# Attention and two matrix chains on one core: W13 built by two blocks of rows at a time, with w_out's last blocks beside it

## Chip, core and metric

The kernel runs on one core of a Trainium2 chip. The metric is the time of one execution in device microseconds (us). TensorE does the matrix products into PSUM, VectorE and ScalarE work on SBUF and PSUM, GpSimd on SBUF, and SyncE's queue (SP) starts most transfers.

## What is computed

Eight batches of 576 tokens with eight heads of 64 go through a two-step attention over 32 packed queries, then through two matrix chains in float32. The part that matters here is the first chain, whose `w3` and `w_out` are multiplied first (W13 = w3 @ w_out), since nothing stands between them:

```python
def sm_attn(qq, kk, vv): ...          # softmax(scale * qq @ kk.T) @ vv
p_packed = sm_attn(p, k, v)
out = sm_attn(q, p_packed, p_packed)
x = out as [4608, 512]
a = x @ w1                            # [4608, 1024]
b = x @ w2
h = a * b @ w3                        # w3 [1024, 1024]
x = h @ w_out                         # w_out [1024, 512]
h = x @ w_in                          # w_in [512, 2048]
g = np.maximum(0.01 * h, h)
return g @ w_out2
```

The weights arrive as 64-bit words and are turned into float32 on the chip.

## The kernel before

TensorE multiplies rounded float32 operands, so each operand is kept as a high and a low part: ScalarE copies the value into the rounded type (high), another engine subtracts (low), and each product takes three passes, high by high, high by low, low by high (`three`, L102). The subtract is one call, `sub` (L107), on the engine that it is given.

The start of the run, some 182 us, is written out by hand in `SCRIPT` (L11), a list of steps. A step is a letter and its indices, looked up in the table at L738. The steps:

- `k q v p` load attention inputs, `s e n t y` are the first attention step, `S E N` the second, `X`/`x` split its result into the tile AT (L258), `X` with the subtract on VectorE and `x` on GpSimd.
- `l`, `c`, `d` bring in a block of weights by the key `w` (w1, w2), `o` (w_out) or `3` (w3): `l` loads 64-bit words into one of three c64 tiles on SP's queue (L292), `c` begins the conversion, one operation on ScalarE (L276) and two on VectorE (L278, L282), and `d` ends it with an addition on GpSimd (L285). The words then lie in one of six c32 tiles until they are split.
- `o`/`O` split a block of w_out into two tiles of 256 columns (`split_wo1`, L508), `H`/`h` a block of w3 into one wsp tile of 512 columns, of which there are four (`split_half`, L386); the capital O and the small h are on GpSimd, the others on VectorE.
- `M` and `a` make M, w1 and w2 folded with the packed attention (L423, L437); `A` followed by the indices fc, batch and half multiplies M with AT into two PSUM tiles, which ScalarE (L473) and VectorE (L475) take out and multiply. The batch 0 and batch 1 results go to memory.
- `W` followed by fc and h is `w13_half` (L519): 24 matmuls over four of w_out's eight blocks, jc 0 to 3 for h = 0 and 4 to 7 for h = 1, into two of the four PSUM tiles named mm. After h = 1 both are copied and split into W13. Block i of w3 is number 2 fc + h, so W10 needs the split H2, and W01 needs H1 and w_out's blocks 4 to 7.

Before, W13 goes from W00 to W01, W10, W20, W30, W21, W11 and so on; all of w_out is split ahead of W00. The kernel is built with `schedule_with_timeline_sim=True` (L1049): the order of instructions on each engine is fixed when the kernel is built, by a planner with modelled times. The script gives the priority; an engine with nothing else to do takes a later step, so the order on an engine can run ahead of the script.

After the script come alternating stages for four pairs of batches (`x2_stage`, `ab_stage`, L767 to L773) and the second chain (L983 on). These are not touched.

Of the kernel before, what the change touches and what calls it, by code (L numbers as in the profile page):

```python
# [7 lines left out]

SCRIPT = """k0 p0 k1 lw0 v0 s0 v1 cw0 e0 q0 n0 s1 q1 t0 e1 lw1 n1 y0 t1 p1 k2 dw0 S0 y1 cw1 k3 v2 E0 S1 s2 v3 dw1 lw2 N0 E1 e2 q2 X0 N1 n2 s3 t2 q3 X1 e3 cw2 lw3 n3 y2 t3 dw2 M00 S2 lw4 a00 y3 cw3 lw5 S3 dw3 Z M01 a01 A000 E2 cw4 lw6 A001 dw4 cw5 E3 dw5 M02 a02 A100 N2 lw7 A101 cw6 x2 M10 a10 A200 N3 dw6 cw7 A201 x3 lw8 dw7 M03 a03 A010 cw8 lw9 A011 dw8 lo0 M11 a11 A300 cw9 lw10 A301 dw9 co0 M04 a04 A110 cw10 lw11 A111 dw10 do0 M12 a12 A400 cw11 lw12 A401 dw11 lo1 O0 M05 a05 A210 cw12 lw13 A211 dw12 co1 M13 a13 A500 cw13 lw14 A501 dw13 lo2 do1 M06 a06 A310 cw14 lw15 A311 dw14 O1 co2 M14 a14 A600 cw15 lo3 A601 dw15 do2 co3 M07 a07 A410 O2 lo4 do3 A411 co4 lo5 M15 a15 A700 O3 l30 do4 A701 co5 lo6 c30 M16 a16 A510 o4 l31 do5 d30 A511 co6 c31 o5 M17 a17 A610 p2 lo7 do6 d31 A611 o6 l33 co7 l35 A710 H0 h1 do7 c33 p3 A711 o7 k4 d33 c35 l32 H3 d35 l37 c32 H5 d32 l34 c37 H2 k5 d37 c34 l38 k6 l315 d34 H4 h7 s4 c38 d38 W00 l36 c36 l39 l310 d36 h6 c39 l311 H8 e4 l312 W01 t4 W10 W20 s5 c311 v4 k7 d39 l313 d311 c310 c312 e5 c313 d310 h9 W30 v5 d312 H11 W21 h10 s6 l314 W11 n4 c314 d313 d314 q4 v7 W31 y4 t5 W40 s7 H12 q5 W41 h13 W50 n5 e6 v6 c315 d315 n6 H14 t6 W51 y5 e7 H15 y6 W60 n7 W61 W70 W71"""  # L11
KQ = {"k": 1}
F32 = mybir.dt.float32
F32R = mybir.dt.float32r
# [18 lines left out]
def tile_kernel(ctx, tc, qT, kT, vL, pT, w12, w3b, wo1, win, wo2, out):  # L33
# [718 lines left out]
    }  # L752
    for x in SCRIPT.split():
        if x[0] in "lcd":
# [298 lines left out]
```

## Time and profile before

| | |
|---|---|
| median of 3 runs | 1363.2 us (1353.9 to 1364.24) |
| profiled execution | 1353.83 us |
| its span, first to last instruction | 1351.5 us |
| TensorE busy | 1314.0 us, 97% |
| VectorE busy | 934.9 us, 69% |
| ScalarE busy | 690.7 us, 51% |
| GpSimd busy | 183.6 us, 14% |
| mean granted TensorE clock | 0.994 |

The profile is of one execution. The page gives busy times of the whole span; the same by stretches of time shows where an engine is full or idle. PE is TensorE's matmul, PEld its weight load, DVE VectorE, ACT ScalarE, POOL GpSimd, SP SyncE. A granted clock of 1.00 is 2.4 GHz, 0.50 is 1.2 GHz. An instruction that waits for a port inside its run shows as a longer instruction, not as idle time.

### The profile page before, as it was taken

To read this page: it belongs to the slowest core of one execution; us is meant where nothing else is said; L and a number is where in the kernel's file an instruction comes from. 1 tells how busy PE (TensorE), PEld (TensorE's weight loads), DVE (VectorE), ACT (ScalarE), POOL (GpSimd) and SP (SyncE) were. 2 spreads that over 40 slices of the span, in tenths; PEclk is the share of its full clock that TensorE was granted. 3 is DMA by queue.
4 is the path that set the end of the run, shared out by engine and by line. 5 is a ranking of instruction groups with operands and counts; after the bars stand their busy time and mean duration, and the time that the engine had idled before them with its cause. 6 is when DMAs were issued, how large, how long until landed. Compare 5 with 4: busy or idle time off the path is not lost. (4 is left out here: it accounts for less than half of the span.)

```text
span 1351.5 us, 23575 instructions
## 1 busy us (share of the span) xinstructions
PE 1314.0 (97%) x8576; PEld 1248.6 (92%) x8576; DVE 934.9 (69%) x1574; ACT 690.7 (51%) x1345; POOL 183.6 (14%) x146
## 2 busy tenths in 40 slices
PE   6998999999999999999999999999999999999998
PEld 3777999999999999999999999999999999999998
DVE  5988558675977587762977665846665468586667
ACT  4554464665476556644665555545334334344432
POOL 1554422332033212100000000000000000000000
PEclk9998999999999999999999999999999999999999
DMA  9788677668976774387878877467545754778884
GB/s 322 266 280 275 210 228 248 222 213 240 311 246 203 255 245 149 111 304 249 296 273 289 305 264 248 160 213 247 186 146 204 242 192 158 268 264 309 285 295 152
DMA packets 174836, 323.48 MB, mean 239 GB/s; under 512 B 22657, under 2 KB 93313, under 8 KB 174721
## 3 DMA queue, kind: packets, MB, share of 16 engines
q1 hardware_dynamic: 153984, 300.74, 66.4%
q10 hardware_dynamic: 20736, 21.24, 4.6%
q8 instruction: 67, 1.10, 0.3%
q14 instruction: 49, 0.39, 0.1%
HBM read 226.75 MB, written 95.16 MB: 238 GB/s over the span
## 5 line engine op out<-in xcount | busy, mean ns | idle before, releaser
L105 PE MATMUL mm<-AT,M 128*128 128x288 f32 x1536 | 230.5, 302 | 9.2 <-DVE ab L475 5.5
L105 PEld LDWEIGHTS mm<-AT,M 128*128 128x128 f32 x1536 | 210.1, 190 | 27.8 <-DVE ab L475 8.1
L908 PE MATMUL b<-xh,wi 128*128 128x384 f32 x768 | 219.2, 338 | 6.3 <-DMA xh<-xfd 3.8
L908 PE MATMUL b<-gh,wo 128*128 128x384 f32 x768 | 213.9, 336 | 1.4 <-DVE o L871 1.4
L105 PEld LDWEIGHTS mm<-ab,W 128*128 128x128 f32 x1536 | 204.3, 188 | 6.7 <-issue 5.2
L105 PE MATMUL mm<-ab,W 128*128 128x288 f32 x1536 | 210.0, 297 | 0.4 <-DVE ab L475 0.4
L908 PEld LDWEIGHTS b<-xh,wi 128*128 128x128 f32 x768 | 141.6, 189 | 8.6 <-DMA xh<-xfd 3.3
L908 PEld LDWEIGHTS b<-gh,wo 128*128 128x128 f32 x768 | 140.3, 188 | 2.1 <-issue 1.0
L908 PE MATMUL b<-xl,wi 128*128 128x384 f32 x384 | 129.3, 337 | 0.0
L908 PE MATMUL b<-gl,wo 128*128 128x384 f32 x384 | 128.6, 335 | 0.0
L680 ACT CAST gh<-gr 128x1152 fp32r<-128x1152 f32 (+1 forms) x72 | 75.6, 1052 | 67.4 <-PE b L908 32.2
L908 PE MATMUL c<-gh,wo 128*128 128x384 f32 x384 | 107.3, 336 | 0.6 <-DVE o L866 0.5
L908 PE MATMUL c<-xh,wi 128*128 128x384 f32 x384 | 106.4, 336 | 1.4 <-DMA xh<-xfd 1.4
L108 DVE TENSOR_TENSOR gl<-gr,gh 128x1152 fp32r<-128x1152 f32 (+1 forms) x72 | 87.4, 1219 | 22.5 <-ACT gh L680 22.5
L285 POOL TENSOR_TENSOR c<-cT,c 128x512 int32<-128x512 int32 x56 | 76.6, 1369 | 158.4 <-DVE cT L282 75.7
L108 DVE TENSOR_TENSOR M<-m,M 64x512 fp32r<-64x512 f32 (+1 forms) x111 | 75.1, 684 | 23.3 <-ACT M L415 19.4
L680 ACT CAST gh<-gs 128x1152 fp32r<-128x1152 f32 (+1 forms) x54 | 56.9, 1055 | 62.7 <-PE b L908 33.5
L108 POOL TENSOR_TENSOR wsp<-wsp 128x512 fp32r<-128x512 f32 x48 | 64.3, 1347 | 160.1 <-ACT wsp L383 138.2
L108 DVE TENSOR_TENSOR ab<-ab,ab 128x288 fp32r<-128x288 f32 x128 | 65.3, 535 | 29.1 <-ACT ab L454 28.6
L856 ACT ACTIVATE gr<-gr 128x1152 f32<-128x1152 f32 (+1 forms) x54 | 57.3, 1062 | 45.8 <-DVE gr L871 45.5
L868 ACT COPY gr<-b 128x384 f32<-128x384 f32 x96 | 45.8, 478 | 60.0 <-PE b L908 58.4
L475 DVE TENSOR_TENSOR ab<-mm,a 128x288 f32<-128x288 f32 x128 | 57.1, 450 | 24.1 <-ACT a L473 12.7
(144 smaller groups left out, 2385.2 us busy)
## 6 DMA issues: line engine op xcount, KB each, us to landing
xh<-xfd SPq DMA_DIRECT2D x126, 384.0 KB, 5.5
xl<-xfd SPq DMA_DIRECT2D x126, 384.0 KB, 5.2
part<-o SPq DMA_DIRECT2D x48, 384.0 KB, 2.8
o<-part SPq DMA_DIRECT2D x48, 384.0 KB, 4.0
c<-wo SPq DMA_DIRECT2D x24, 512.0 KB, 4.6
wsp<-w12d SPq DMA_DIRECT2D x48, 256.0 KB, 3.0
abd<-ab ACTq DMA_DIRECT2D x80, 144.0 KB, 3.0
ab<-abd SPq DMA_DIRECT2D x80, 144.0 KB, 3.9
```

The costliest lines, as they stand in the source:

```text
L105: nc.tensor.matmul(dst, lhs(i), rhs(j), start=first and n == 0, stop=last and n == 2)
L108: engine.tensor_tensor(out=out, in0=x, in1=rd(hi), op=ALU.subtract)
L285: return lambda: nc.gpsimd.tensor_tensor(out=q, in0=t.bitcast(I32), in1=q, op=ALU.add)
L475: nc.vector.tensor_tensor(out=t, in0=pb[:, :TH], in1=a, op=ALU.mult)
L680: nc.scalar.copy(hi[step], x[step])
L856: nc.scalar.activation(out=out, in_=x, func=AF.Prelu, alpha=0.01)
L868: nc.scalar.copy(out, ps)
L908: nc.tensor.matmul(dst, lhs(l), rhs(r), start=first and n == 0, stop=last and n == total - 1, skip_group_check=True)
```

## The change

Only `SCRIPT` differs. Both scripts have 305 steps with the same loads, conversions, products and splits.

- X2 and X3 in place of x2 and x3, o0 to o3 in place of O0 to O3: these subtracts go from GpSimd to VectorE. H1 in place of h1, and ahead of A711 besides H0 now H2 and H1. Of the sixteen w3 splits three are on GpSimd (h5, h10, h11), before six (h1, h6, h7, h9, h10, h13).
- W13's order is W00 W10 W01 W11, W20 W30 W21 W31, W40 W50 W41 W51, W60 W70 W61 W71. The w3 blocks are loaded, converted and split in this order.
- The loads, conversions and splits of w_out's blocks 4 to 7 (lo4, co4, do4, o4 and on) stand between those of the first four w3 blocks; co7, do7 and o7 come behind W00.
- The steps of the next batches' attention (k4, s4, e4 and on) stand at other places among the W steps.

```diff
 ... dw5 M02 a02 A100 N2 lw7 A101 cw6
-x2 M10 a10 A200 N3 dw6 cw7 A201 x3 lw8 dw7 M03
+X2 M10 a10 A200 N3 dw6 cw7 A201 X3 lw8 dw7 M03
...
-O0 M05 a05 A210 cw12 lw13 A211 dw12 co1 M13 a13 A500 cw13 lw14 A501 dw13 lo2 do1 M06 a06 A310 cw14 lw15 A311 dw14 O1 co2 M14
+o0 M05 a05 A210 cw12 lw13 A211 dw12 co1 M13 a13 A500 cw13 lw14 A501 dw13 lo2 do1 M06 a06 A310 cw14 lw15 A311 dw14 o1 co2 M14
...
-A410 O2 lo4 do3 A411 co4 lo5 M15 a15 A700 O3 l30 do4 A701 co5 lo6 c30
-M16 a16 A510 o4 l31 do5 d30 A511 co6 c31 o5 M17 a17 A610 p2 lo7 do6 d31 A611 o6 l33 co7 l35
-A710 H0 h1 do7 c33 p3 A711 o7 k4 d33 c35 l32 H3 d35 l37 c32 H5 d32 l34 c37 H2 k5 d37 c34
-l38 k6 l315 d34 H4 h7 s4 c38 d38 W00 l36 c36 l39 l310 d36 h6 c39 l311 H8 e4 l312 W01 t4 W10 W20
-...
-s7 H12 q5 W41 h13 W50 n5 e6 v6 c315 d315 n6 H14 t6 W51 y5 e7 H15 y6 W60 n7 W61 W70 W71
+A410 o2 l30 do3 A411 c30 l32 M15 a15 A700 o3 d30 c32 A701 lo4 H0 l31
+M16 a16 A510 d32 co4 lo5 A511 do4 H2 c31 M17 a17 A610 o4 p2 co5 d31 l33 A611 do5 lo6 c33
+A710 o5 H1 co6 d33 p3 A711 W00 do6 lo7 o6 H3 k4 l34 co7 W10 do7 l36 c34 o7 k5 d34 W01
+H4 c36 l35 s4 d36 W11 H6 e4 k6 c35 l37 d35 W20 h5 t4 c37 l38 s5 v4 d37 W30 H7 e5 c38 l310 k7 d38 W21
+...
+H14 y5 e7 v7 c313 l315 d313 W60 H13 y6 c315 n7 d315 W70 H15 W61 W71
```

## Rows read from the trace of the kernel before

**Rows 1.** The page's first part: busy us, share of the span, instructions of each engine.

```profile
PE 1314.0 (97%) x8576; PEld 1248.6 (92%) x8576; DVE 934.9 (69%) x1574; ACT 690.7 (51%) x1345; POOL 183.6 (14%) x146
```

**Rows 2.** Busy time by stretches: start:end, length, each engine's busy us, PEclk, DMA share, GB/s.

```profile
40.00:64.00 24.00, 23.01 (x163) 19.02 (x162) 23.80 (x45) 12.70 (x28) 12.93 (x10) 0.98 0.75 260
64.00:93.00 29.00, 26.75 (x187) 21.43 (x186) 21.07 (x33) 15.11 (x36) 18.14 (x16) 1.00 0.83 271
93.00:112.00 19.00, 17.14 (x117) 13.22 (x115) 19.00 (x31) 12.19 (x28) 11.15 (x9) 1.00 0.80 258
112.00:117.00 5.00, 2.33 (x15) 1.84 (x14) 5.00 (x8) 1.07 (x3) 2.13 (x2) 0.92 0.97 313
117.00:123.00 6.00, 6.00 (x22) 4.59 (x24) 5.97 (x10) 2.99 (x6) 2.62 (x2) 0.50 0.97 349
126.50:182.00 55.50, 55.50 (x476) 51.58 (x475) 28.54 (x57) 27.25 (x67) 20.42 (x15) 1.00 0.64 207
```

**Rows 3.** Groups of instructions, 38 to 126.5 us: busy us, mean ns, idle before.

```profile
L105 PE MATMUL mm<-AT,M 128*128 128x288 f32 x384 | 61.6, 312 | 7.8 <-DVE ab L475 4.1 <-DVE M L108 2.5 <-POOL AT L108 1.0
L282 DVE SCALAR_TENSOR_TENSOR cT<-c,cT 128x512 uint32<-128x512 uint32 x27 | 24.7, 913 | 0.2
L285 POOL TENSOR_TENSOR c<-cT,c 128x512 int32<-128x512 int32 x16 | 21.6, 1352 | 21.5 <-DVE cT L282 15.4 <-ACT a L473 4.3 <-ACT M L440 1.8
L278 DVE TENSOR_SCALAR cT<-c 128x512 uint32<-128x512 uint32 x26 | 19.2, 740 | 4.7 <-DMA c<-wo 3.7 <-DMA c<-w 1.0
L285 POOL TENSOR_TENSOR w<-cT,w 128x512 int32<-128x512 int32 x11 | 15.9, 1463 | 13.1 <-ACT w L276 6.9 <-DMA w12d<-w 2.7 <-DVE cT L282 1.8
L108 POOL TENSOR_TENSOR ab<-c,ab 128x256 fp32r<-128x256 f32 x8 | 7.0, 894 | 3.1 <-ACT ab L513 3.1
L108 DVE TENSOR_TENSOR ab<-c,ab 128x256 fp32r<-128x256 f32 x8 | 5.8, 748 | 0.0
L108 POOL TENSOR_TENSOR AT<-a,AT 128x576 fp32r<-128x576 f32 x2 | 3.0, 1511 | 0.5 <-ACT AT L261 0.5
L108 POOL TENSOR_TENSOR wsp<-c,wsp 128x512 fp32r<-128x512 f32 x1 | 1.8, 1752 | 0.0
```

**Rows 4.** Timeline where TensorE waits: start us, us, engine, line, operation, idle before.

```profile
55.77 0.68 ACT L261 CAST AT<-a 128x576 fp32r<-128x576 f32 x1
56.43 1.30 DVE L278 TENSOR_SCALAR cT<-c 128x512 uint32<-128x512 uint32 x1
57.40 1.60 POOL L108 TENSOR_TENSOR AT<-a,AT 128x576 fp32r<-128x576 f32 x1
59.05 1.31 PE L105 MATMUL mm<-AT,M 128*128 128x288 f32 x8 [0.99 <-POOL AT L108]
...
93.02 0.60 DVE L108 TENSOR_TENSOR ab<-c,ab 128x256 fp32r<-128x256 f32 x1
...
111.00 1.83 DVE L108 TENSOR_TENSOR ab<-c,ab 128x256 fp32r<-128x256 f32 x2
113.83 1.58 PE L105 MATMUL mm<-AT,M 128*128 128x288 f32 x10 [1.13 <-DVE M L108]
114.52 1.59 POOL L285 TENSOR_TENSOR c<-cT,c 128x512 int32<-128x512 int32 x1 [1.97 <-DVE cT L282]
114.90 1.49 DVE L278 TENSOR_SCALAR cT<-c 128x512 uint32<-128x512 uint32 x1
116.81 3.25 PE L105 MATMUL mm<-AT,M 128*128 128x288 f32 x12 [1.40 <-DVE ab L475]
```

**Rows 5.** Timeline of VectorE at 104 us, with no GpSimd instruction beside these.

```profile
104.19 0.41 DVE L278 TENSOR_SCALAR cT<-c 128x512 uint32<-128x512 uint32 x1
104.52 0.41 DVE L108 TENSOR_TENSOR ab<-c,ab 128x256 fp32r<-128x256 f32 x1
105.22 0.68 DVE L282 SCALAR_TENSOR_TENSOR cT<-c,cT 128x512 uint32<-128x512 uint32 x1
```

**Rows 6.** Timeline of TensorE inside the W13 stage.

```profile
134.22 8.29 PE L105 MATMUL mm<-ab,wsp 128*128 128x256 f32 x68
```

More of the change, by code (lines that the diff above doesn't have):

```diff
@@ L7 @@
 from concourse.masks import make_identity
-SCRIPT = """k0 p0 k1 lw0 v0 s0 v1 cw0 e0 q0 n0 s1 q1 t0 e1 lw1 n1 y0 t1 p1 k2 dw0 S0 y1 cw1 k3 v2 E0 S1 s2 v3 dw1 lw2 N0 E1 e2 q2 X0 N1 n2 s3 t2 q3 X1 e3 cw2 lw3 n3 y2 t3 dw2 M00 S2 lw4 a00 y3 cw3 lw5 S3 dw3 Z M01 a01 A000 E2 cw4 lw6 A001 dw4 cw5 E3 dw5 M02 a02 A100 N2 lw7 A101 cw6 x2 M10 a10 A200 N3 dw6 cw7 A201 x3 lw8 dw7 M03 a03 A010 cw8 lw9 A011 dw8 lo0 M11 a11 A300 cw9 lw10 A301 dw9 co0 M04 a04 A110 cw10 lw11 A111 dw10 do0 M12 a12 A400 cw11 lw12 A401 dw11 lo1 O0 M05 a05 A210 cw12 lw13 A211 dw12 co1 M13 a13 A500 cw13 lw14 A501 dw13 lo2 do1 M06 a06 A310 cw14 lw15 A311 dw14 O1 co2 M14 a14 A600 cw15 lo3 A601 dw15 do2 co3 M07 a07 A410 O2 lo4 do3 A411 co4 lo5 M15 a15 A700 O3 l30 do4 A701 co5 lo6 c30 M16 a16 A510 o4 l31 do5 d30 A511 co6 c31 o5 M17 a17 A610 p2 lo7 do6 d31 A611 o6 l33 co7 l35 A710 H0 h1 do7 c33 p3 A711 o7 k4 d33 c35 l32 H3 d35 l37 c32 H5 d32 l34 c37 H2 k5 d37 c34 l38 k6 l315 d34 H4 h7 s4 c38 d38 W00 l36 c36 l39 l310 d36 h6 c39 l311 H8 e4 l312 W01 t4 W10 W20 s5 c311 v4 k7 d39 l313 d311 c310 c312 e5 c313 d310 h9 W30 v5 d312 H11 W21 h10 s6 l314 W11 n4 c314 d313 d314 q4 v7 W31 y4 t5 W40 s7 H12 q5 W41 h13 W50 n5 e6 v6 c315 d315 n6 H14 t6 W51 y5 e7 H15 y6 W60 n7 W61 W70 W71"""
@@ new lines @@
+SCRIPT = """k0 p0 k1 lw0 v0 s0 v1 cw0 e0 q0 n0 s1 q1 t0 e1 lw1 n1 y0 t1 p1 k2 dw0 S0 y1 cw1 k3 v2 E0 S1 s2 v3 dw1 lw2 N0 E1 e2 q2 X0 N1 n2 s3 t2 q3 X1 e3 cw2 lw3 n3 y2 t3 dw2 M00 S2 lw4 a00 y3 cw3 lw5 S3 dw3 Z M01 a01 A000 E2 cw4 lw6 A001 dw4 cw5 E3 dw5 M02 a02 A100 N2 lw7 A101 cw6 X2 M10 a10 A200 N3 dw6 cw7 A201 X3 lw8 dw7 M03 a03 A010 cw8 lw9 A011 dw8 lo0 M11 a11 A300 cw9 lw10 A301 dw9 co0 M04 a04 A110 cw10 lw11 A111 dw10 do0 M12 a12 A400 cw11 lw12 A401 dw11 lo1 o0 M05 a05 A210 cw12 lw13 A211 dw12 co1 M13 a13 A500 cw13 lw14 A501 dw13 lo2 do1 M06 a06 A310 cw14 lw15 A311 dw14 o1 co2 M14 a14 A600 cw15 lo3 A601 dw15 do2 co3 M07 a07 A410 o2 l30 do3 A411 c30 l32 M15 a15 A700 o3 d30 c32 A701 lo4 H0 l31 M16 a16 A510 d32 co4 lo5 A511 do4 H2 c31 M17 a17 A610 o4 p2 co5 d31 l33 A611 do5 lo6 c33 A710 o5 H1 co6 d33 p3 A711 W00 do6 lo7 o6 H3 k4 l34 co7 W10 do7 l36 c34 o7 k5 d34 W01 H4 c36 l35 s4 d36 W11 H6 e4 k6 c35 l37 d35 W20 h5 t4 c37 l38 s5 v4 d37 W30 H7 e5 c38 l310 k7 d38 W21 H8 n4 c310 l39 s6 v5 d310 W31 h10 y4 q4 t5 c39 l311 d39 W40 H9 s7 v6 c311 l312 q5 d311 W50 h11 n5 e6 c312 l314 d312 W41 H12 t6 c314 l313 n6 d314 W51 H14 y5 e7 v7 c313 l315 d313 W60 H13 y6 c315 n7 d315 W70 H15 W61 W71"""
```

## The prediction

> **What bounds the kernel now.** I read the page's first part, then busy time by stretches, then one table of instruction groups for the script's part of the run, and last the timelines of the places where TensorE waits. The page shows TensorE busy 97% of the span, so no other engine can be the bound over the whole [rows 1]. By stretches the loss is found in one place: ahead of 117 us TensorE is idle in every stretch read, most from 93 on, while in the W13 stage, 126.5 to 182, it is busy 55.50 of 55.50 [rows 2]. The reader should see two things in that table. First, the stage that the change reorders most (W13) has no idle TensorE time to give back. Second, ahead of it VectorE is full: 23.80 of 24 us, later 19.00 of 19, 5.00 of 5, 5.97 of 6; only from 64 to 93 has it 7.9 us free.
>
> The table of groups names who TensorE waits for between 38 and 126.5: 7.8 us in all, 4.1 for L475 (the product that empties a's and b's PSUM tiles), 2.5 for the subtract that makes M's low part, both on VectorE, and 1.0 for a subtract on GpSimd [rows 3]. So VectorE, not TensorE, sets the pace there. And VectorE is stretched by GpSimd: L282 takes 0.913 us in the mean and 0.68 alone, L278 0.740 and 0.41 alone [rows 3, 5]. The worst place is 112 to 117, where TensorE is busy 2.33 of 5 us; right behind it, 117 to 123, the granted clock is 0.50, that is 1.2 instead of 2.4 GHz, though TensorE is busy all of it [rows 2]. The idle time (2.67 us) and half of the slow stretch (3.0 us) make 5.7 us lost at one spot. Of the rest of the idle time, 0.99 us is the wait for GpSimd's X3 [rows 4]. The idle time before 40 us stays out: the two scripts are the same up to cw6.
>
> **The splits that move to VectorE.** X2 and X3 are one subtract of 128x576 each, o0 to o3 two of 128x256 each, H1 one of 128x512. Alone, VectorE takes 0.41 us for 256 columns and 0.68 for 512 [rows 5]; 576 columns by the same slope are an estimated 0.75 (the 512 columns are L282's, which also reads two operands from SBUF). The sum added ahead of W00: 2 x 0.75 + 8 x 0.41 + 0.68 = 5.5 us. The ScalarE copies that come before each subtract stay where they are. GpSimd loses 3.0 + 7.0 + 1.8 = 11.8 us of the same work [rows 3].
>
> What does VectorE get back? Its L278, L282 and o-splits are stretched by 26 x 0.33 + 27 x 0.233 + 8 x 0.338 = 17.6 us, over GpSimd's 21.6 + 15.9 + 7.0 + 3.0 + 1.8 = 49.3 us of work, or 0.36 us for each us of GpSimd [rows 3, 5]. 11.8 us less gives back 4.2 us. Net, VectorE gets 1.3 us more, at bounds of 5.5 more (nothing comes back, since the 27 additions of L285 stay and may do the blocking instead) and 6.3 less (each us of GpSimd blocks one). I take 1.3, from the mean over 49 us. By place: X2, X3 and o0 fall into the full stretch up to 64 and there add 2.3 us against some 5 us of GpSimd taken away (1.8 back); o1 to o3 add 2.5 us where 7.9 us are free; H1's 0.68 stands against 1.8 us of GpSimd (0.6 back). So I count the net at nothing in TensorE's time. The cover is the free time from 64 to 93; without it the 1.3 us would be paid one to one.
>
> One row bears on how the blocking works: L278 at 114.90 takes 1.49 us instead of 0.41 while GpSimd adds from 114.52 to 116.11 [rows 4, 5]. The Trainium skill, "SBUF — State Buffer", section "Who interferes with whom", says that VectorE and GpSimd share a port pair that one of them holds for a whole instruction, while the other is blocked. The row agrees; by the rule alone VectorE could win back up to 11.8 - 5.5 = 6.3 us, by the mean it loses 1.3.
>
> **X3's own wait.** A010 and A011 want the AT tile's low part at 58.06 (59.05 less the 0.99 of idle time) and get it at 59.05, since GpSimd begins X3 only at 57.40, though its copy is done at 56.45 [rows 4]. On VectorE X3 would be ready at 56.45 too; VectorE is then inside a stretched L278 until 57.7, so X3 would end about 58.4. TensorE then waits 0.4 instead of 1.0: 0.6 us gained, bounds 0 and 1.0.
>
> **w_out's last four.** co4 to co7 and o4 to o7 go from ahead of the w3 blocks to among them, co7 and o7 to between W10 and W01. Work per block is the same, loads and SP issues too: 12 loads of 512 KB stand ahead of k4's in either script, so SP's queue reaches the second half's k, v, q loads no later. What matters is what VectorE does at 109 to 117. There it runs o7's two subtracts, 1.83 us, right ahead of the M split for which A610 waits 1.13 us, then a stretched L278 ahead of the two L475 for which A611 waits 1.40 us [rows 4]. With o7 gone from this spot, M's split could start up to 1.8 us earlier; that would take A610's wait away and perhaps the slow clock, up to 5.7 us. Against it: the planner lets VectorE run ahead of the script, as o4's first subtract shows, at 93.02, though the script has it behind M16 and A510, while A610's matmuls run at 113.83 [rows 4, 5]. So the next conversion or H split would fill the gap, with its own GpSimd addition behind it. Bounds 0 and 5.7; I take 2, nearer the low end because of that row.
>
> **W13's new order.** W00 W10 W01 W11 needs H0, H2, then o4 to o7 with H1, H3. Each W is 24 matmuls of 8.29 us / 68 = 0.122, so 2.9 us; the stage's 384 run without idle time today [rows 2, 6]. Two blocks hold all four "mm" tiles, so W10 waits for A711's last L475, hidden by W00, and W20 waits for fc 0's two copies and two subtracts, the subtracts 0.41 us each [rows 5], hidden by W11's 2.9 us. Without that cover two subtracts a pair would show, 0.8 us, 3.3 in all four pairs. Four wsp tiles hold H0, H2, H1 and H3 and come free one W at a time, as they do today. Cost: 0, no gain either.
>
> **Sum.** 0 - 0.6 - 2.0 + 0 = -2.6 us. The profiled execution's own time is 1353.8 (span 1351.5), so 1351.2 for it. The median of the runs shown, 1363.2, lies 9.4 us above the profiled one, inside their spread (1353.9 to 1364.2); for the median I say 1360.6.
>
> **The rivals.**
> - The stall clears. Without o7 and with fewer GpSimd instructions, 112 to 123 runs at full clock: -0.6 - 5.7 = -6.3, with all waits of the stretch gone at most -7.8 - 3.0 = -10.8. For it: the 1.83 us stand right before the first wait. Against: VectorE stays full. 1357 (1352 at the least).
> - Slower: VectorE is the bound ahead of W13 and the 5.5 us are paid. It decides when less than 5.5 / 11.8 = 0.47 us comes back for each us taken off GpSimd and no free time lies beside it; the trace has 0.36, so net it goes that way by 1.3 us, and only the free time from 64 to 93 hides it. If nothing comes back: +5.5, and with the slow clock as long again +3.0: +8.5, 1371.7. The Trainium skill, "Perfetto Trace Analysis", section "Identifying the Most-Contended Engine", has the busiest engine relieved first; by this VectorE, full in four stretches, is the wrong engine to load. The rows agree on which engine is full.
> - W01 starves: o7's chain (load, conversion, addition, two subtracts) is last in line and W01 stands still until it ends. Two W ahead of it instead of one give 5.9 us of cover rather than 2.9; o7's subtracts end at 112.8 today [rows 4], so it would have to come 19 us later to cost anything (126.5 + 5.9 - 112.8 = 19.6); at 30 us later 10.4 us are lost, with a slow-clock stretch of 3: 1377.
> - The change does little: the planner runs ahead of the script in both, and the same GpSimd additions fall on the same VectorE work: 1363.
>
> **How the numbers follow.** Small gain 0.45, stall clears 0.17, no difference 0.13, VectorE pays 0.18, W01 starves 0.07. The likeliest gives 1360.6, by itself 1357 to 1363. The range takes in the stall clearing with runs at the low end of their spread (1353.9 - 5 = 1349) and VectorE paying nearly in full (1370); the rest is left out. A change of under 1% (13.6 us) is about what a measurement of this kernel can't tell from none. No case but W01 starving passes that by itself; all idle time and slow clock together are 10.8 us. Faster by over 1% needs the clearing case and low runs: 0.07. Slower by over 1%: W01, or VectorE paying with a longer slow stretch: 0.07. Within: 0.86.
>
> **What would show it.** X3: no GpSimd AT subtract, and A010's wait under 0.5 us. Splits: GpSimd near 37 us instead of 49 between 38 and W00, L278 and L282 closer to 0.41 and 0.68. w_out: o7 behind W00's start, and the clock of the stretch ahead of W00 at 1.00 (gain) or 0.50 again (none). W13: TensorE busy throughout. I am wrong if TensorE idles inside W13, if the wait sum ahead of W00 goes over 10 us, or if something moves behind 182 us, which I left as it is.

## The result

The changed kernel takes 1371.3 us in the median of 13 runs (1364.5 to 1376.4) beside 1361.9 us of the kernel before in 13 runs (1353.9 to 1367.1). The ratio is 1.007, with a 95% interval of 1.0052 to 1.0087: about 9.4 us slower. The prediction said 1360.6 us and a range of 1349 to 1370, so the direction was wrong and the time lies above the range, though it is still within 1%. The interval also shows that this measurement can tell 0.7% from nothing, which the prediction doubted.

The profiled execution of the kernel before was among its fastest, that of the changed kernel a middling one (span 1368.9 us). The two profiles therefore lie 17.4 us apart, more than the kernels do. 4.6 us of this lie ahead of A000, which starts at 40.2 us before and at 44.8 us after. The kernels below that have unit 4 (explained further down) at the front, before among them, start A000 anywhere from 40.2 to 45.0 us, so this part doesn't go with it. Another 6.1 us lie behind the second pair's M, where no step was moved; that stretch takes 1114 to 1126 us in the sixteen profiles, with no clear tie to the order.

The first part of the page, and busy time by stretches (columns as in [rows 2]; the last two rows are the W13 stage and the first x2 stage):

```profile
PE 1316.3 (96%) x8576; PEld 1248.4 (91%) x8576; DVE 949.4 (69%) x1587; ACT 690.3 (50%) x1345; POOL 167.1 (12%) x133
```

```profile
60.00:64.00 4.00, 1.15 (x10) 0.45 (x6) 4.00 (x3) 1.49 (x5) 3.46 (x3) 1.00 0.99 275
64.00:67.00 3.00, 1.59 (x10) 1.36 (x10) 3.00 (x9) 0.74 (x2) 0.00 (x0) 0.85 0.99 381
67.00:73.00 6.00, 5.00 (x20) 3.69 (x20) 4.22 (x9) 0.93 (x3) 0.00 (x0) 0.50 0.13 42
...
112.00:117.00 5.00, 4.21 (x29) 3.36 (x30) 4.97 (x8) 3.06 (x7) 2.57 (x2) 1.00 0.69 216
117.00:123.00 6.00, 5.11 (x31) 3.30 (x28) 5.94 (x11) 2.21 (x7) 2.55 (x2) 1.00 0.88 282
132.70:187.92 55.22, 54.66 (x467) 51.19 (x465) 37.19 (x67) 28.09 (x65) 20.58 (x15) 1.00 0.69 222
187.92:248.37 60.45, 57.74 (x443) 52.85 (x442) 45.32 (x81) 28.73 (x73) 12.79 (x9) 1.00 0.73 234
```

The first x2 stage before, in the same view:

```profile
181.83:237.13 55.30, 55.30 (x421) 51.62 (x420) 45.01 (x82) 27.88 (x67) 15.65 (x10) 1.00 0.84 259
```

The stall of 112 to 123 us is gone: TensorE is busy 4.21 of 5 and 5.11 of 6 us at full clock, where before it had 2.33 us and then 6 us at 0.50 [rows 2]. But a new stall of the same kind stands at 60 to 73 us. TensorE is busy 2.74 of 7 us, and behind that the granted clock is 0.50 (1.2 GHz) for 6 us. And the first x2 stage, which was full, is now 5.2 us longer and has 2.7 us of idle time. The W13 stage is as long as it was.

The places where TensorE waits in the changed kernel (start us, us, engine, line, operation, idle before):

```profile
50.53 3.44 PE L105 MATMUL mm<-AT,M 128*128 128x288 f32 x22 [0.77 <-DVE M L108]
64.13 1.59 PE L105 MATMUL mm<-AT,M 128*128 128x288 f32 x10 [2.98 <-DVE AT L108]
67.18 1.33 PE L105 MATMUL mm<-AT,M 128*128 128x288 f32 x4 [1.46 <-ACT AT L261]
69.33 2.29 PE L105 MATMUL mm<-AT,M 128*128 128x288 f32 x8 [0.82 <-DVE AT L108]
...
146.15 1.68 PE L105 MATMUL mm<-ab,wsp 128*128 128x256 f32 x12 [0.56 <-DVE W L108]
200.39 0.33 PE L219 MATMUL at<-ident,pp 128*128 128x128 f32 x1 [1.48 <-ACT pp L218]
```

A010 and A011 now wait 5.26 us in three pieces for batch 1's AT (L261 copies it, L108 makes the low part), where before one wait of 0.99 us stood [rows 4]. In the same stretch of the kernel before, there is something else on TensorE and on SP's queue, which the prediction's rows don't show:

```profile
34.02 0.33 SPq L129 DMA_DIRECT2D raw<-kT  x1
...
45.46 1.19 PE L167 MATMUL at<-raw,ppad 128*64 128x288 f32 x8
55.09 0.75 PE L198 MATMUL at<-ident,P 128*128 128x128 f32 x4
55.68 0.27 PE L199 MATMUL at<-ident,P 128*64 128x128 f32 x1
```

These are k4, s4 and t4: the loads, scores and transpositions of attention unit 4, the first of the second pair of batches. In the script before, k4 and s4 stand ahead of W00 and t4 behind it, but the planner ran them some 70 to 90 us ahead of W00's start, among the first A steps. In the changed kernel the loads come at 112.87 us and the scores at 119.47 us. The script of the change puts k4 to t4 up to three W later, and the planner no longer takes them to the front.

### The profile page after: what moved, and what is told of

Its sections match the earlier page's. It is cut to its first block, busy times and chain, and to the rows that moved or that the text cites. A ratio compares the mean times of both kernels' runs of the same rounds, so it can differ in the third digit from the quotient of the medians.

```text
span 1368.9 us, 23566 instructions
## 1 busy us (share of the span) xinstructions
PE 1316.3 (96%) x8576; PEld 1248.4 (91%) x8576; DVE 949.4 (69%) x1587; ACT 690.3 (50%) x1345; POOL 167.1 (12%) x133
## 4 chain that ended last, share of the span: by engine, by line
PE 75%; DMA 12%; DVE 9%; ACT 2%; issue 2%; SPq 1%; POOL 0%; ACTq 0%; DVEq 0%; POOLq 0%
PE mm L105 25%; PE b L908 24%; PE c L908 12%; PE a L908 6%; DMA xh<-xfd 3%; PE m L105 2%; PE at L167 2%; DMA part<-o 2%; DMA wsp<-w12d 2%; DVE cT L278 1%; PE at L216 1%; DMA wi<-wid 1%; DMA c<-w 1%; DMA xfd<-PT 1%; DVE cT L282 1%
## 5 line engine op out<-in xcount | busy, mean ns | idle before, releaser
L105 PE MATMUL mm<-AT,M 128*128 128x288 f32 x1536 | 230.9, 301 | 17.3 <-DVE ab L475 4.4
L105 PEld LDWEIGHTS mm<-AT,M 128*128 128x128 f32 x1536 | 209.0, 189 | 37.7 <-issue 8.1
L105 PE MATMUL mm<-ab,W 128*128 128x288 f32 x1536 | 211.1, 296 | 1.2 <-DVE ab L108 0.9
L105 PEld LDWEIGHTS mm<-ab,W 128*128 128x128 f32 x1536 | 204.6, 188 | 8.0 <-issue 6.3
L108 DVE TENSOR_TENSOR gl<-gr,gh 128x1152 fp32r<-128x1152 f32 (+1 forms) x72 | 87.4, 1218 | 22.1 <-ACT gh L680 22.0
L108 DVE TENSOR_TENSOR ab<-ab,ab 128x288 fp32r<-128x288 f32 x128 | 66.9, 549 | 45.1 <-ACT ab L454 44.5
L108 DVE TENSOR_TENSOR M<-m,M 64x512 fp32r<-64x512 f32 (+1 forms) x111 | 75.3, 686 | 20.8 <-ACT M L415 16.4
L108 POOL TENSOR_TENSOR wsp<-wsp 128x512 fp32r<-128x512 f32 x48 | 62.2, 1303 | 172.7 <-ACT wsp L383 142.8
L908 PEld LDWEIGHTS c<-xh,wi 128*128 128x128 f32 x384 | 69.9, 188 | 5.0 <-DMA xh<-xfd 4.3
```

Source lines behind the costliest of these rows:

```text
L105: nc.tensor.matmul(dst, lhs(i), rhs(j), start=first and n == 0, stop=last and n == 2)
L108: engine.tensor_tensor(out=out, in0=x, in1=rd(hi), op=ALU.subtract)
L908: nc.tensor.matmul(dst, lhs(l), rhs(r), start=first and n == 0, stop=last and n == total - 1, skip_group_check=True)
```

## The experiments

All differ from one of the two kernels in the order of `SCRIPT` or the engine of a few splits only; the work is the same. Each time is the median of 6 to 13 runs, the ratio is to the kernel before on the same chip, with its 95% interval. "Unit 4" is the start of its scores, and "A to M" the time from A000's first product to the second pair's M, both from one profiled execution.

| kernel | us | ratio | unit 4, us | A to M, us |
|---|---|---|---|---|
| before, beside after | 1361.9 | 1 | 45.5 | 196.9 |
| after | 1371.3 | 1.0070 (1.0052 to 1.0087) | 119.5 | 203.5 |
| x_only | 1360.4 | 1.0004 (0.9990 to 1.0019) | 47.3 | 195.7 |
| o_only | 1358.2 | 0.9975 (0.9958 to 0.9992) | 48.5 | 193.6 |
| order_only | 1369.2 | 1.0060 (1.0036 to 1.0083) | 116.0 | 202.2 |
| after_x | 1367.5 | 1.0057 (1.0037 to 1.0076) | 116.4 | 206.3 |
| w_order | 1361.9 | 1.0021 (1.0002 to 1.0039) | 49.7 | 200.7 |
| wout_early | 1369.0 | 1.0081 (1.0057 to 1.0106) | 142.5 | 202.1 |
| att_old | 1356.0 | 0.9977 (0.9961 to 0.9993) | 47.2 | 191.6 |
| att_new | 1366.2 | 1.0053 (1.0035 to 1.0070) | 139.7 | 202.3 |
| grp_early | 1354.6 | 0.9962 (0.9944 to 0.9980) | 49.9 | 190.8 |
| rest_early | 1366.2 | 1.0042 (1.0023 to 1.0061) | 117.9 | 199.1 |
| unit4_early | 1356.9 | 0.9978 (0.9962 to 0.9995) | 47.3 | 191.4 |
| grp_late | 1371.4 | 1.0082 (1.0062 to 1.0101) | 137.6 | 203.0 |
| k4_ahead_lo7 | 1356.4 | 0.9979 (0.9958 to 1.0001) | 45.7 | 194.7 |
| k4_behind_l32 | 1362.7 | 1.0022 (1.0007 to 1.0036) | 119.3 | 199.1 |

**First: are the splits to blame?** x_only and o_only make one part of the change alone, on the kernel before.

```diff
 x_only, on before
-x2 ... x3
+X2 ... X3
 o_only, on before
-O0 ... O1 ... O2 ... O3
+o0 ... o1 ... o2 ... o3
```

> The kernel before with X2 and X3 on VectorE and nothing else changed. Theory A (the AT chain comes late: with X2 and X3 on VectorE, the changed kernel's TensorE waits 2.98 + 1.46 + 0.82 us for AT ahead of A010 and A011): 4 to 7 us slower than before, with AT waits of 3 us or more. Theory B (VectorE pays for the subtracts that it takes over, each microsecond one to one): 1.5 us slower. Theory C (the loss comes from the order of the W13 steps and of what stands beside them): no difference, within 1 us.

> The kernel before with o0 to o3 on VectorE and nothing else changed. Theory A: no difference, within 1 us. Theory B: 3.3 us slower, and VectorE full for longer ahead of W00. Theory C: no difference.

X2 and X3 on VectorE change nothing that can be measured. The wait for X3, though, grew: x_only has 1.81 us where before it was 0.99 us [rows 4], so the 0.6 us of the prediction aren't there either. ScalarE's copy is done at 60.85 us, but VectorE comes to the subtract only at 62.20, behind two L278, and it takes 1.27 us beside a GpSimd split:

```profile
60.17 0.68 ACT L261 CAST AT<-a 128x576 fp32r<-128x576 f32 x1 [2.50 <-DVE a L255]
61.22 1.63 POOL L108 TENSOR_TENSOR ab<-c,ab 128x256 fp32r<-128x256 f32 x2 [0.85 <-ACT ab L513]
62.20 1.27 DVE L108 TENSOR_TENSOR AT<-a,AT 128x576 fp32r<-128x576 f32 x1
63.52 1.31 PE L105 MATMUL mm<-AT,M 128*128 128x288 f32 x8 [1.81 <-DVE AT L108]
```

o0 to o3 on VectorE gain 3.4 us (0.25%, 1 to 6 by the interval), and in o_only's profile the clock stays at 1.00 from 112 to 128 us. order_only and after_x take the splits back out of the changed kernel:

```diff
 order_only, on after          after_x, on after
-X2 X3 o0 o1 o2 o3            -X2 X3
+x2 x3 O0 O1 O2 O3            +x2 x3
```

> The changed kernel with x2, x3 and O0 to O3 back on GpSimd: the new order of W13, of w_out's last four blocks and of the attention steps, with H1 on VectorE, remains. Theory A: as the kernel before within 2 us. Theory B: 0.7 us slower than before (H1). Theory C: 5 to 9 us slower than before, with TensorE waiting in the first 20 us behind W13 (1.48 us for pp, 0.93 and 0.29 for ab in the changed kernel).

> The changed kernel with x2 and x3 back on GpSimd and nothing else undone. Theory A: 4 to 7 us faster than the changed kernel, so 2 to 5 us slower than before. Theory B: 1.5 us faster than the changed kernel, so 8 slower than before. Theory C: as the changed kernel, 9 us slower than before.

Both stay at 1.006, so neither theory about VectorE holds: the loss is in the order. The AT waits shrink (in after_x from 5.26 to 0.80 us in all), yet the time hardly moves: after_x idles 5.40 us in the first x2 stage, where the changed kernel idles 2.71.

**Then: which part of the order?** Three things were reordered: the W steps with their w3 blocks, w_out's last four blocks, and the attention steps. w_order takes only the first into the kernel before, att_new only the last. att_old and wout_early undo one part in the changed kernel, by putting each step beside the same count of W steps as before.

```diff
 att_old, on after
-A711 W00 do6 lo7 o6 H3 k4 l34 co7 W10 ... o7 k5 d34 W01 ... s4 d36 W11 H6 e4 k6
+A711 k4 k5 k6 s4 W00 do6 lo7 o6 H3 l34 e4 co7 W10 do7 l36 t4 c34 o7 d34 W01 ...
```

> The kernel before with W13 by two blocks of rows, first halves first, and w3's blocks brought in in that order; w_out's blocks, the attention steps and the engines of the splits by place as before. Theory C1 (W13's order costs): 5 to 9 us slower than before, with TensorE waiting 2 us or more in the 20 us behind W13. C2 (w_out's last four blocks beside w3's cost) and C3 (the new places of the attention steps cost): as before within 2 us, no wait behind W13.

> The changed kernel with the next batches' attention steps (k4, s4, v7, y6 and so on) beside the same number of W steps as in the kernel before; all else changed. C3: 5 to 9 us faster than the changed kernel, no wait behind W13. C1 and C2: as the changed kernel within 2 us, with the ScalarE cast of a w12d word (L383) waiting 5 us or more for its transfer right behind W13.

> The kernel before with the attention steps beside the same number of W steps as in the changed kernel; W13's order, w_out and the splits as before. C3: 5 to 9 us slower than before, TensorE waiting 2 us or more behind W13. C1 and C2: as before within 2 us.

> The changed kernel with w_out's last four blocks as early as in the kernel before; W13's new order, the new places of the attention steps and the splits on VectorE remain. C2: 5 to 9 us faster than the changed kernel. C1 and C3: as the changed kernel within 2 us, with TensorE waiting 2 us or more behind W13.

The attention's places carry the loss. Moved back, they turn 1.007 into 0.9977; moved alone, they turn 1 into 1.0053. W13's new order costs at most 0.4%, and w_out's place has no share that shows (it was moved back only beside a late unit 4).

Theory C3 has the right steps, but not the right place. It put the wait behind W13; att_new has none there, and idles 12.9 us ahead of W13 instead of 7.8. The wait behind W13 came in w_order, as C1 has it, though with a smaller loss than C1's. The first x2 stage of w_order, with ScalarE's wait for a w12 block and TensorE's wait behind it:

```profile
184.61:245.51 60.90, 57.55 (x421) 53.24 (x420) 43.38 (x75) 28.28 (x67) 15.39 (x11) 0.97 0.73 236
```

```profile
194.06 0.62 ACT L383 CAST wsp<-wsp 128x512 fp32r<-128x512 f32 x1 [5.00 <-DMA wsp<-w12d]
195.34 0.75 PE L198 MATMUL at<-ident,P 128*128 128x128 f32 x4 [3.19 <-ACT ppM L223]
```

**Then: which attention steps?** 18 of them have moved. grp_early puts ten back (k4 to k7, s4, e4, t4, s5, v4, e5), rest_early the other eight, unit4_early only k4, s4, e4, t4; grp_late moves the ten alone on the kernel before.

> The changed kernel, with ten attention steps alone at the kernel before's places: k4, k5, k6, k7, s4, e4, t4, s5, v4, e5, which the change put up to three W later. Theory G (these steps are the cause: one unit of attention less is done before W13 and in its early part, and comes due behind it): the ratio to the kernel before falls from the changed kernel's 1.007 to 0.996 to 0.999, the first x2 stage from 60.4 us to about 55.3, TensorE's waits in it from 2.7 us to under 0.5. Theory V (v7, y6 and the other eight late steps are the cause, since they delay the last loads and products of the attention): stays at 1.005 to 1.008, the x2 stage at about 60.

> The changed kernel, with the other eight moved attention steps alone at the kernel before's places (s6, v5, q4, v6, n5, e6, v7, y6). Theory G: nothing changes, 1.005 to 1.008, first x2 stage about 60 us. Theory V: 0.996 to 0.999, stage 55.3 us.

> The changed kernel, with only the four steps of attention unit 4 (k4, s4, e4, t4) at the kernel before's places. Theory G in its narrow form (that one unit of attention is missing ahead of the first x2 stage): most of the group's gain comes with these four, ratio 0.997 to 1.001. Theory G in its wide form (it is the whole chain of k loads and scores that must be early): 1.003 to 1.006. Theory V: 1.005 to 1.008.

> The kernel before, with the group of ten attention steps (k4, k5, k6, k7, s4, e4, t4, s5, v4, e5) alone at the changed kernel's places. Theory G: 1.004 to 1.007, first x2 stage some 2 to 5 us longer than 55.3, or as many us of idle TensorE ahead of W13. Theory V: 0.999 to 1.001.

Theory G holds in its narrow form: four steps of unit 4 bring back 0.92% of the time. rest_early, at 1.0042 and with a first x2 stage of 57.8 us, lies a little better than theory G had it (1.005 and 60 us). TensorE's timeline where A010 waits, grp_early first (unit 4's and 5's scores, then A010), then rest_early:

```profile
49.88 1.19 PE L167 MATMUL at<-raw,ppad 128*64 128x288 f32 x8
63.05 1.19 PE L167 MATMUL at<-raw,ppad 128*64 128x288 f32 x8
64.50 1.33 PE L105 MATMUL mm<-AT,M 128*128 128x288 f32 x8 [0.26 <-DVE AT L108]
```

```profile
63.01 1.59 PE L105 MATMUL mm<-AT,M 128*128 128x288 f32 x10 [2.27 <-DVE AT L108]
66.06 1.33 PE L105 MATMUL mm<-AT,M 128*128 128x288 f32 x4 [1.47 <-ACT AT L261]
68.21 2.29 PE L105 MATMUL mm<-AT,M 128*128 128x288 f32 x8 [0.82 <-DVE AT L108]
```

Up to here all kernels with unit 4's scores at 45 to 50 us are at 0.996 to 1.002, all with them at 116 us or later at 1.004 to 1.008, whatever engine their splits are on.

**Last: one step.** In the order that the planner fixes (for two of these scripts read without a run) k4's loads jump to the front or don't, and one step decides: on the changed script they jump with k4 ahead of lo7 and don't behind it, on the script before they jump with k4 ahead of l32 and don't behind it. lo7 and l32 are each one more load of a weight block on SP's queue ahead of k4's.

```diff
 k4_ahead_lo7, on after
-W00 do6 lo7 o6 H3 k4 l34 co7 W10
+W00 do6 k4 lo7 o6 H3 l34 co7 W10
 k4_behind_l32, on before
-A711 o7 k4 d33 c35 l32 H3
+A711 o7 d33 c35 l32 k4 H3
```

> The changed kernel with one step moved: k4 from behind H3 to ahead of lo7, three steps earlier; s4, t4 and all else stay at their places. In the order fixed for this script k4's loads and unit 4's scores stand among the first A steps again. Theory F (what was lost is unit 4's work that filled TensorE's waits at 45 to 60 us): the scores run at 45 to 50 us, A010 waits under 2.5 us in all instead of 5.3, ratio 0.996 to 1.001. Theory P (the group's place behind W13's start costs the time): ratio 1.004 to 1.008, and the first x2 stage stays at about 60 us.

> The kernel before with one step moved: k4 from ahead of d33 to behind l32, four steps later, all else as it was. In the order fixed for this script k4's loads and unit 4's scores no longer stand among the first A steps. Theory F: ratio 1.003 to 1.008, waits ahead of AT for A010 and A011 of over 2 us. Theory P: 0.999 to 1.001, since the other nine steps of the group stay.

k4_ahead_lo7's queue and TensorE, and its W13 and x2 stages:

```profile
35.30 0.33 SPq L129 DMA_DIRECT2D raw<-kT  x1
...
45.69 1.19 PE L167 MATMUL at<-raw,ppad 128*64 128x288 f32 x8
56.05 0.75 PE L198 MATMUL at<-ident,P 128*128 128x128 f32 x4 [0.19 <-ACT P L182]
61.40 2.29 PE L105 MATMUL mm<-AT,M 128*128 128x288 f32 x8 [2.63 <-DVE AT L108]
```

```profile
124.66:177.40 52.74, 52.74 (x455) 50.15 (x454) 33.17 (x63) 27.12 (x62) 19.73 (x15) 1.00 0.70 229
177.40:235.55 58.15, 57.13 (x442) 52.70 (x441) 45.41 (x80) 28.34 (x71) 13.18 (x9) 1.00 0.75 240
```

One step, three places earlier, takes the changed kernel from 1.0070 to 0.9979: some 12 us (9 to 16 by the two intervals), as much as the whole loss or more. Theory F is borne out there, except that A010 still waits 2.63 us, not under 2.5. On the kernel before the same kind of move, three places later, costs 0.22%, 3 us. That is less than the 0.3% at which theory F began and more than theory P allowed; the interval, 1.0007 to 1.0036, touches both. Its waits are as F has them:

```profile
63.70 0.80 PE L105 MATMUL mm<-AT,M 128*128 128x288 f32 x4 [1.44 <-ACT AT L261]
66.37 2.29 PE L105 MATMUL mm<-AT,M 128*128 128x288 f32 x8 [1.86 <-POOL AT L108]
119.29 1.14 PE L167 MATMUL at<-raw,ppad 128*64 128x288 f32 x8
```

So in both scripts the kernel is slower with unit 4 late; how much that is worth depends on the rest of the order. In k4_behind_l32 the other nine steps still stood early (unit 5's scores follow at 136 us, in the changed kernel only at 151.56 us), and with all ten late the loss is 0.82% (grp_late). With k4_behind_l32 at 1.0022 and w_order at 1.0021 the two groups of kernels touch.

## Where the time goes

The changed kernel and k4_ahead_lo7 do the same work from A000 to the second pair's M, and differ by one step of the script. 203.5 less 194.7 makes 8.8 us. 6.8 of them are idle time of TensorE (13.98 us against 7.20), the other 2.0 a longer busy time, 1.3 of it in the A products (61.7 us against 60.4 in the groups). The halved clock doesn't tell the two apart: k4_ahead_lo7 has such a stretch too, behind its wait for AT.

```profile
60.70:67.50 6.80, 6.10 (x24) 4.69 (x25) 4.88 (x10) 2.62 (x6) 0.56 (x1) 0.50 0.40 149
```

Over all the kernels the idle time from A000 to M goes with unit 4's place: 5.3 to 8.3 us where it is early (w_order 12.0), 10.2 to 14.0 where it is late. In the changed kernel and k4_ahead_lo7 it falls in these places:

- From A000 to A011 the changed kernel idles 6.47 us: 0.77, 0.23 and 0.21 for M and for a product's exit, and 2.98, 1.46 and 0.82 for AT. k4_ahead_lo7 idles 2.82 us there (0.19 and 2.63), although it does unit 4's scores and transpositions on top (1.19, 0.75 and 0.27 us).
- From there to W00 the difference is 0.9 us, inside W13 0.6, and in the first x2 stage 1.7.

The AT wait is the larger piece. The subtract's engine has a part in it, since after_x, with X2 and X3 on GpSimd, waits only 0.80 us for AT; but that gains no time, and k4_ahead_lo7 has both subtracts on VectorE and waits half as long. From the transposition of the last scores (L238) to the end of X2's subtract VectorE takes 20.1 us in the changed kernel (44.02 to 64.07) and 12.0 in k4_ahead_lo7 (40.01 to 51.96). In the changed kernel's order more of other work stands in between: five L278 and five L282 against four and three, three M splits against two, and one more step of X3's chain; several of them are stretched. The last steps ahead of that end, on GpSimd and VectorE of the changed kernel:

```profile
58.76 2.97 POOL L285 TENSOR_TENSOR w<-cT,w 128x512 int32<-128x512 int32 x2 [6.12 <-DVE st L252]
61.69 1.77 POOL L285 TENSOR_TENSOR c<-cT,c 128x512 int32<-128x512 int32 x1
60.52 1.82 DVE L253 TENSOR_TENSOR sT<-sT,st 128x576 f32<-128x576 f32 x1
62.26 1.81 DVE L108 TENSOR_TENSOR AT<-a,AT 128x576 fp32r<-128x576 f32 x1
```

X2's subtract (62.26) stands behind a step of X3's chain (60.52), and beside GpSimd's additions, which run from 58.76 to 63.5, the two take 1.82 and 1.81 us. In k4_ahead_lo7 X2's subtract starts at 51.27 us, with no addition of GpSimd beside it, and takes 0.69.

Behind W13 a chain of queues shows. SP's queue, ScalarE and TensorE of the changed kernel:

```profile
188.81 6.26 SPq L488 DMA_DIRECT2D ab<-abd  x9
195.16 0.38 SPq L378 DMA_DIRECT2D wsp<-w12d  x1
199.45 0.62 ACT L383 CAST wsp<-wsp 128x512 fp32r<-128x512 f32 x1 [5.23 <-DMA wsp<-w12d]
199.98 0.36 ACT L218 ACTIVATE pp<-at,st 128x128 f32<-128x128 f32 x1
```

The load of a w12 block stands behind nine reloads on SP's queue; ScalarE waits 5.23 us for it, and in ScalarE's order the attention's pp (L218) stands behind that wait, for which TensorE waits 1.48 us at 200.39. In the kernel before that load is issued at 185.10 us, there too behind eight reloads, and ScalarE waits 1.74 us. w_order, with unit 4 early, has the same chain as the changed kernel (5.00 and 3.19 us above), so it is not unit 4's place alone that makes it. That the reloads' place is the cause was not tried alone.

## Why the prediction was wrong, step by step

**The step that failed.** It is the sentence that "12 loads of 512 KB stand ahead of k4's in either script, so SP's queue reaches the second half's k, v, q loads no later", together with what it left uncosted: the moved attention steps. The count was right and the conclusion wrong. In the trace of before k4's loads are at 34.02 us, ahead of all 12. The prediction knew that the planner runs ahead of the script (o4's first subtract at 93.02 [rows 4]), used this against a gain, and didn't ask which steps already ran ahead and could lose it. A look at where each moved step ran would have shown unit 4 at 45 us. Price: 1.0070 against 0.9979, some 12 us.

**"The two scripts are the same up to cw6", so idle time before 40 us stays out.** The scripts are, the orders aren't: k4's loads leave SP's queue at 34 us though k4 stands 130 steps behind cw6. The same holds for "if something moves behind 182 us, which I left as it is": the first x2 stage grew by 5.2 us. All three signs by which the prediction would know itself wrong came: this one, 0.56 us of idle time inside W13, and a wait sum over 10 us.

**The splits.** Net nothing, hidden: right in its result. x_only measured no change (1.0004) and o_only -3.4 us, so loading the fuller engine gave a small gain. The rival in which VectorE pays 5.5 us falls by the same two runs (H1 was not tried alone); that the o-splits gain because they leave an engine that stretches VectorE is likely, not shown. The Trainium skill, "Perfetto Trace Analysis", section "Identifying the Most-Contended Engine", has the busiest engine optimized first; what the prediction's rival drew from it, that VectorE was the wrong engine to load, isn't borne out by these two runs. The groups of the changed kernel from 38 to 132.7 us, as in [rows 3]:

```profile
L105 PE MATMUL mm<-AT,M 128*128 128x288 f32 x384 | 61.7, 309 | 12.0 <-DVE AT L108 3.8 <-DVE ab L475 3.6 <-DVE M L108 1.5
L282 DVE SCALAR_TENSOR_TENSOR cT<-c,cT 128x512 uint32<-128x512 uint32 x28 | 22.0, 787 | 0.3
L278 DVE TENSOR_SCALAR cT<-c 128x512 uint32<-128x512 uint32 x27 | 20.9, 775 | 3.2 <-DMA c<-wo 2.6 <-DMA c<-w 0.7
L285 POOL TENSOR_TENSOR c<-cT,c 128x512 int32<-128x512 int32 x14 | 18.9, 1349 | 23.2 <-DVE cT L282 14.2 <-ACT M L440 4.5 <-ACT c L276 2.6
L285 POOL TENSOR_TENSOR w<-cT,w 128x512 int32<-128x512 int32 x13 | 18.0, 1396 | 34.5 <-ACT w L276 18.5 <-DVE st L252 6.1 <-DVE cT L282 3.8
L108 DVE TENSOR_TENSOR ab<-c,ab 128x256 fp32r<-128x256 f32 x16 | 8.3, 544 | 0.0
L108 DVE TENSOR_TENSOR wsp<-c,wsp 128x512 fp32r<-128x512 f32 x4 | 4.3, 1072 | 0.0
L108 DVE TENSOR_TENSOR AT<-a,AT 128x576 fp32r<-128x576 f32 x2 | 2.6, 1278 | 0.0
```

GpSimd is at 18.9 + 18.0 = 36.9 us, as foretold (near 37). Counted on the instructions that stood in the prediction's sum, L278, L282 and eight o-splits are now stretched by 26 x 0.365 + 27 x 0.107 + 8 x 0.134 = 13.4 us instead of 17.6. So about 4.1 us came back, where 4.2 were counted. L282 went toward 0.68 us, L278 didn't go toward 0.41. Too good was the price of the subtracts that moved, since they are stretched as well: in the mean X2 and X3 take 1.28 us instead of 0.75, an o-split 0.54 instead of 0.41, a w3 split 1.07 instead of 0.68. That makes 2.6 + 8 x 0.544 + 1.07 = 8.0 us where 5.5 were counted, and a net of some 3.9 us instead of 1.3. The wait sum of L105 is 12.0 us, over the 10 that the prediction named as its own refutation.

**X3's wait.** A gain of 0.6 us was counted; x_only's wait grew from 0.99 to 1.81 us, the changed kernel's to 5.26. The step assumed that VectorE comes to X3 after one stretched L278 and runs it at its own pace. In x_only two L278 stand ahead of it and it takes 1.27 us; in the changed kernel VectorE's whole order ahead of A010 is another.

**w_out's last four.** "The stall clears" is what happened at its place: 112 to 123 us runs at full clock. The rival's total didn't follow, because 60 to 73 us got a stall of its own, with the same halved clock. Nor is its mechanism shown. o_only runs 112 to 123 at 1.00 too, with w_out's blocks where they were, so the late o7 isn't needed for it. x_only, with o7 and the o-splits as before, keeps the two waits of before, 1.13 and 1.40 us there, and has no halved clock from 112 to 128 us:

```profile
117.56 1.58 PE L105 MATMUL mm<-AT,M 128*128 128x288 f32 x10 [1.14 <-DVE M L108]
120.55 1.87 PE L105 MATMUL mm<-AT,M 128*128 128x288 f32 x12 [1.40 <-DVE ab L475]
```

So the 3.0 us of slow clock, which the prediction priced as part of this stall, needn't come with it. And wout_early, with w_out's blocks early again, is no faster than the changed kernel.

**W13's order.** "Cost 0, no gain": w_order has +0.21% (0.02 to 0.39), 2.9 us by the ratio. The stage itself is as foretold: TensorE is busy without a gap in w_order's W13 (0.56 us idle in the changed kernel's). The loss shows behind it, which the prediction left out: w_order's first x2 stage takes 60.90 us instead of 55.30 and holds 3.35 us of idle time, 3.19 of it the one wait shown above.

With k4 back at the front the whole change measures 0.9979 (0.9958 to 1.0001), that is -2.9 us; the sum of the prediction was -2.6. Its terms don't earn that agreement one by one, as the points above show.

**What stays open.** Why one load more ahead of k4's in the script keeps the planner from lifting them wasn't found. Nor was it settled how the 12 us divide between unit 4's own work, which fills waits, and VectorE's different order around AT: both come and go with the same step. And the same move is worth some 12 us in one script and 3 in the other.

The lowest ratio is grp_early's, 0.9962 (0.9944 to 0.9980; the intervals of four others overlap it): some 5 us faster than the kernel before by the ratio, and by the two ratios 1.1% faster than the changed kernel.

## What to carry to other kernels

When a planner fixes the order, a step's place in the source isn't its time: look up in the trace where each moved step runs today, above all those that run far ahead of their place and fill the bound engine's waits, and count what is lost when they no longer do. A part of a diff that looks like bookkeeping gets a row of its own. And where a change mixes an engine swap with a reordering, run each alone first: here the swap was worth 0 and -3 us, and one step of the order 12 in one script and 3 in the other.

## What was not expected of the hardware

- Taking 12.4 us of work off GpSimd (49.3 to 36.9 us) gave the same VectorE conversions and splits back 4.1 us, a third of a us for each us, and the subtracts that went over to VectorE took 2.5 us longer than alone. The Trainium skill's rule of the shared port ("SBUF — State Buffer", "Who interferes with whom") agrees with single rows, such as the two VectorE steps at 60.52 and 62.26 above (1.82 and 1.81 us, without GpSimd beside them 0.74 and 0.69). But the swap took away 4.1 us of stretching and brought 2.5 of its own: 27 additions stay on GpSimd, before and after.
- The halved clock came behind a stall, but not behind each. Before, TensorE idled 2.67 us from 112 to 117 and then ran 6 us at 0.50 [rows 2]; after, it idled 4.26 us from 60 to 67 and then ran at 0.50 from 67 to 73, busy 5.00 us of it. Half of that busy time, an estimated 3.0 and 2.5 us, came on top of the idle time. But x_only has the stall of 112 to 117 us unchanged (1.14 and 1.40 us, shown above) and none of the slow clock, and unit4_early waits 2.35 us for AT at 62.76 and stays at 1.00 from 60 to 72.
